# A planned attention and gated-MLP kernel: transposes and quarter loads planned in order of issue, one copy moved, all queues ordered anew

## The chip, the cores and the metric

The kernel runs on one NeuronCore of a Trainium2 chip. The metric is device time in microseconds; the time before is the median of three runs. TensorE is called PE below, VectorE DVE, ScalarE ACT, GpSimd POOL, and SP is the engine that issues most DMAs.

## The reference

The input x has 2048 rows of 512 bf16 numbers. After a LayerNorm without scale, two branches start from the same xn. The first is attention with 32 heads of 16, in which each row looks at 8 rows: itself and those 2, 4, ... 14 before it. The second is a gated MLP of width 1792. The output joins them.

```
xn = layernorm(x)
q, k, v = split(xn @ wqkv)                     # 32 heads of 16
logits[h, s, w] = q[h, s] . k[h, s - 2*w] / 4  # w = 0..7, masked where s - 2*w < 0
o[h, s] = sum over w of softmax(logits)[h, s, w] * v[h, s - 2*w]
s = o @ wo
g = silu( (gelu(xn @ w_gate) * (xn @ w_up)) @ w_down )
out = x + s * g
```

## The kernel before, in words

**Blocks.** The 2048 rows are cut into four blocks of 512 (j = 0 to 3) and sixteen tiles of 128 (t = 0 to 15). For each block the kernel does a LayerNorm, a transpose of xn to columns (`xT`), q, k and v projections, the windowed logits and softmax, the weighted sum of v, the two wide projections gate and up (14 groups of four matmuls each), the down projection (four tiles of 14 matmuls, in pieces of 4, 4, 4 and 2), the output projection (four groups of four matmuls), and the final gating and residual.

**Who does what.** PE does the projections, and the transposes of block 0's four tiles. The transposes of blocks 1 to 3 are DMA transposes on SP's queue (line 393). ACT evicts nearly every PSUM bank (q, k, v at lines 489 and 554 to 563, gelu at 907, up at 915, silu at 973, the output at 1032), takes the exponentials, and for blocks 2 and 3 also the row sums of the LayerNorm (lines 347 and 353). DVE does the products and adds of the attention (741, 754, 834 and around), the gated products (929) and the final gating. POOL issues the stores and loads of v and DMAs that accumulate halves of products (763, 857).

**Through DRAM.** q, k, v and the attention output of a block are stored to DRAM and loaded in another layout: a quarter load brings 128 positions to 32 partitions, so four quarter loads (`ldq`, `ldk` on SP, lines 600 and 618, `ldv` on POOL, line 636) fill a block's tile. `sto` (990) and `ldo` (999) do the same for the attention output, which the output projection reads. Block 0 is apart: its projections go tile by tile (16 matmuls of 128 columns, line 541), so that PE can start after the first tile, and its q and k are used straight from SBUF.

**Tile 0 to 3 at the start.** Each tile is normalised by DVE, transposed by PE into a PSUM bank (`turn`, line 329) and copied into `xT0` (`copy`). The copy of tile 1 is DVE's (line 336), those of tiles 0, 2 and 3 are ACT's (lines 442 and 338).

**What sets the order.** The kernel is written as a list of named operations. Each has an engine, a planned duration, the operations it needs, the buffers it takes and uses, and a priority. `schedule` runs through this list with a model of the engines and queues and picks, for each engine, the ready operation that can start first (within 0.05 us the one of lowest priority number). The result is one order per engine, and the instructions are issued in exactly that order; engines and queues then work in order, and wait on semaphores only for data and buffers. The priorities come from per-block offsets (`N`, `Q`, `S`, `V`, `F`, `Y`, `O` for LayerNorm, projections, logits, values, gate and up, down, output) and from `nudge`, a list with one number for each operation, a tenth of which is added to its priority. The same buffer slots that the plan gives out are used on the chip: six PSUM banks (`F`), one double bank (`L`) for the first two tiles of a down projection, five stores' buffers (`vst`) that the evictions of q, k and v fill in turn, and so on.

**Needs and landings.** In `schedule` an operation becomes ready when all that it needs are done; for a DMA that is its landing. A block's second to fourth transpose name the block's first transpose among their needs, and a block's second to fourth quarter load the first one, because the first takes the buffer:

```
self.op(f"copy{t}", "SP", 1.25, [f"norm{t}"] + ([f"copy{t - tt}"] if tt else []), cross, ...)
need = [f"st_q{j}_{c}" for c in range(NC)] + ([f"ldq{j}_0"] if tq else [])
```

So the plan holds them until the first has landed. **The loads** (`loads`) are a sequence of their own on SP, with priorities from -1000 up, but for the last three (`late=3`: w_down, block 3's x, wo), which need block 1's last norm and have priority 0 and up.

Of the kernel before, what the change touches and what calls it, by code (L numbers as in the profile page):

```python
# [27 lines left out]

B, S, D, DF = 1, 2048, 512, 1792
NC = D // P  # L30
# [24 lines left out]
PARAMS = dict(  # L55
    sums=(2, 3), ladd=2, ln_act=4, warm=4, slack=1.65, N=[-229.9, -416.4, 944.9, 875.4],
    S=[589.3, 14.8, 227.7, 124.2], V=[198.8, 530.8, 849.2, -424.8], Q=[-621.6, -708.7, -247.0, -608.9],
    F=[118.2, 189.7, 347.4, 1042.3], Y=[156.3, 30.0, 947.7, 479.9], O=[-160.4, 783.0, 575.9, 952.0], lsum=(0,),
    late=3, vsum=(0, 1),
    nudge=[  # L60
# [39 lines left out]
    ],  # L100
# [16 lines left out]
def schedule(ops, pools):  # L117
    by = {o.name: o for o in ops}
    assert len(by) == len(ops)
    waits, nexts = {}, {o.name: [] for o in ops}  # L120
    for i, o in enumerate(ops):
        o.n = i
        waits[o.name] = len(o.need)
        for d in o.need:
            nexts[d].append(o.name)
    users = {}
# [17 lines left out]
    while any(ready.values()):  # L144
        best = None
        for e, rs in ready.items():
# [3 lines left out]
            for o in rs:  # L150
                t = max(clock[e], at[o.name])
                ok = True
                if o.take:
                    p, n = o.take[0][0], len(o.take)
                    ok = len(free[p]) >= n
                    if ok:
                        t = max(t, heapq.nsmallest(n, free[p])[-1][0])
# [46 lines left out]
        for n in nexts[o.name]:  # L204
            waits[n] -= 1
            if not waits[n]:
                at[n] = max(
                    by[d].done if by[d].eng == by[n].eng else by[d].end + by[n].slack for d in by[n].need
                )
                ready[by[n].eng].append(by[n])  # L210
# [4 lines left out]
class Kernel:  # L215
# [52 lines left out]
    def layernorm(self, j):  # L268
        base = self.when("N", j)
        for tt in range(TPB):  # L270
# [60 lines left out]
            def copy(t=t, tt=tt, j=j):  # L331
                if tt == 0:
                    self.new(f"xT{j}", [P, NC, TQ], BF16, "xnT")
                out = self.t[f"xT{j}"][:, :, tt * P : (tt + 1) * P]
                if t == 1:
                    self.nc.vector.tensor_copy(out=out, in_=self.t[f"tr{t}"][:])
                else:
                    self.nc.scalar.activation(out=out, in_=self.t[f"tr{t}"][:], func=AF.Copy)
# [49 lines left out]
            if j:  # L388

                def cross(t=t, tt=tt, j=j):  # L390
                    if tt == 0:
# [4 lines left out]

                self.op(f"copy{t}", "SP", 1.25, [f"norm{t}"] + ([f"copy{t - tt}"] if tt else []), cross,
                        take=[("xT", f"xT{j}")] if tt == 0 else [], use=[f"xn{t}", f"xT{j}"], prio=prio,
# [5 lines left out]
            need = [f"turn{t}"] + ([f"copy{t - tt}"] if tt else [])  # L404
            self.op(f"copy{t}", *(("DVE", 0.34) if t == 1 else ("ACT", 0.5)), need, copy, take=take, use=[f"tr{t}", f"xT{j}"], prio=prio)

# [184 lines left out]
    def q_loads(self, j):  # L591
        for tq in range(TPB):
# [11 lines left out]

            need = [f"st_q{j}_{c}" for c in range(NC)] + ([f"ldq{j}_0"] if tq else [])
            self.op(f"ldq{j}_{tq}", "SP", 0.6, need, load, take=[("q", f"q{j}")] if tq == 0 else [],
                    use=[f"q{j}"], prio=1.0, nbytes=260 * 1024, kind="ld")

    def k_loads(self, j):
        for tq in range(TPB):  # L610
# [13 lines left out]
            need += [f"st_k{j - 1}_{c}" for c in range(NC)] if j > 1 else ["st_k0"]  # L624
            need += [f"ldk{j}_0"] if tq else []
            self.op(f"ldk{j}_{tq}", "SP", 0.6, need, load, take=[("k", f"k{j}")] if tq == 0 else [],
                    use=[f"k{j}"], prio=1.0, nbytes=290 * 1024, kind="ld")

    def v_loads(self, j):
        for tq in range(TPB):  # L630
# [11 lines left out]
            if j == 0:  # L642
                need = [f"st_v0_{t}" for t in range(tq + 1)]
            need += [f"ldv{j}_0"] if tq else []
            self.op(f"ldv{j}_{tq}", "POOL", 0.7, need, load, take=[("v", f"v{j}")] if tq == 0 else [],
# [453 lines left out]
    def loads(self, src):  # L1099
# [45 lines left out]
        for i, (name, fn, nbytes) in enumerate(seq):  # L1145
            late = [f"norm{2 * TPB - 1}"] if i >= len(seq) - self.par["late"] else []
            self.op(name, "SP", 0.35, late, fn, prio=(0.0 if late else -1000.0) + i, nbytes=nbytes)

# [117 lines left out]
```

## Time and profile before

| | us |
|---|---|
| median of three runs | 218.44 (216.86 to 218.99) |
| the profiled execution: its time | 218.16 |
| its span in the trace | 216.5 |
| granted TensorE clock, mean | 0.997 |
| PE busy | 207.4 |
| DVE busy | 183.3 |
| ACT busy | 151.4 |
| POOL busy | 44.2 |

The span is the time from the first to the last instruction in the trace of one execution; its time as measured from outside is 1.66 us more. A matmul's busy time is modelled and includes its way through the pipeline (a 512-column matmul shows 379 ns, while the next starts 216 ns after it), so the starts tell more than the busy share. A timeline line gives start, time, engine, line, operation, out<-in and, in brackets, how long the engine stood idle before it and what released it. A line of waits gives who waited for whom, the total, how often, and the longest.

### The profile page before, as it was taken

The numbers are of one execution on the slowest core, as the hardware profiler recorded it, in microseconds if no ns is written. First come the engines' busy times: TensorE is split into PE (matmuls) and PEld (weight loads), VectorE is DVE, ScalarE is ACT, GpSimd is POOL, SyncE is SP. The second block draws the span as 40 slices with busy tenths as digits, with TensorE's granted clock in tenths as the row PEclk, the third lists the DMA queues.
The fourth block names the chain that finished last, engine by engine and source line by source line (L and its number), as shares of the span: only waits on it lengthen the run. The fifth ranks groups of instructions, "written<-read, shape, count | busy, mean of one in ns | idle before, by whom it ended". The sixth has DMA issues, their size and how long they took to land.

```text
span 216.5 us, 3096 instructions
## 1 busy us (share of the span) xinstructions
PE 207.4 (96%) x1108; PEld 99.5 (46%) x1108; DVE 183.3 (85%) x211; ACT 151.4 (70%) x264; POOL 44.2 (20%) x76
## 2 busy tenths in 40 slices
PE   7989999799999999999999999999998999999991
PEld 2986443244444444444444444444443444444440
DVE  4597996499869999789999999997999979999114
ACT  3568999979977997973444797766722787675351
POOL 5209110207091203047001004430210000300000
PEclk9999999999999999999999999999999999999998
DMA  5999999738999944699904638999327052553922
GB/s 161 362 375 358 191 237 307 118 126 206 233 160 246 197 117 140 172 190 232 171 0 97 145 116 225 215 201 188 65 48 181 0 98 96 100 97 65 225 99 97
DMA packets 48623, 36.02 MB, mean 166 GB/s; under 512 B 29904, under 2 KB 45408, under 8 KB 48608
## 3 DMA queue, kind: packets, MB, share of 16 engines
q1 hardware_dynamic: 44240, 23.99, 44.8%
q0 software_dynamic: 4224, 11.78, 26.4%
q8 instruction: 8, 0.13, 0.3%
q14 instruction: 7, 0.06, 0.1%
q10 hardware_dynamic: 144, 0.07, 0.1%
HBM read 17.44 MB, written 9.47 MB: 124 GB/s over the span
## 4 chain that ended last, share of the span: by engine, by line
PE 87%; ACT 4%; DMA 3%; DVE 3%; issue 1%; SPq 0%; DVEq 0%
PE y_ps L955 22%; PE u_ps L891 20%; PE g_ps L891 20%; PE qkv_ps L478 14%; PE s_ps L1018 5%; PE qkv_ps L541 5%; DMA xnT<-xn 2%; DMA x_sb<-in_A_x_dram 1%; ACT gl L907 1%; ACT hT L915 1%; DVE s L1069 1%; ACT junk L347 1%; ACT junk L353 1%; DVE s L1075 1%; DVE stats L413 0%
## 5 line engine op out<-in xcount | busy, mean ns | idle before, releaser
L891 PE MATMUL u_ps<-xnT,wu_sb 128*128 128x512 bf16 x224 | 54.2, 379 | 0.0
L891 PE MATMUL g_ps<-xnT,wg_sb 128*128 128x512 bf16 x224 | 53.9, 379 | 0.0
L955 PE MATMUL y_ps<-wd_sb,hT 128*128 128x512 bf16 x224 | 50.3, 379 | 0.7 <-ACT sil L973 0.7
L907 ACT ACTIVATE gl<-g_ps 128x512 bf16<-128x512 f32 x56 | 32.1, 597 | 15.8 <-PE g_ps L891 11.6
L915 ACT ACTIVATE hT<-u_ps 128x512 bf16<-128x512 f32 x56 | 32.6, 597 | 11.0 <-PE u_ps L891 10.8
L834 DVE TENSOR_TENSOR pv<-attn,v_arr 128x4096 bf16<-128x4096 bf16 x16 | 36.0, 2288 | 0.1
L955 PEld LDWEIGHTS <-hT 128*128 128x128 bf16 x224 | 21.8, 98 | 27.6 <-issue 1.0
L891 PEld LDWEIGHTS <-wu_sb 128*128 128x128 bf16 x224 | 21.9, 98 | 26.4
L891 PEld LDWEIGHTS <-wg_sb 128*128 128x128 bf16 x224 | 21.9, 98 | 26.2
L741 DVE TENSOR_TENSOR prod<-q_sb,k_sb 128x4096 bf16<-128x4096 bf16 x12 | 27.1, 2288 | 3.7 <-DMA k_sb<-kT_dram 2.5
L489 ACT ACTIVATE qkv_st<-qkv_ps 128x512 bf16<-128x512 f32 x36 | 20.6, 598 | 3.2 <-PE qkv_ps L478 3.1
L754 DVE TENSOR_TENSOR prod<-prod 128x1024 bf16<-128x1024 bf16 (+2 forms) x33 | 22.6, 738 | 0.0
L929 DVE TENSOR_TENSOR hT<-hT,gl 128x1024 bf16<-128x1024 bf16 x28 | 18.8, 688 | 2.2 <-ACT hT L915 1.5
L973 ACT ACTIVATE sil<-y_ps 128x512 bf16<-128x512 f32 x16 | 8.8, 596 | 14.0 <-PE y_ps L955 13.9
L857 POOL DMA_DIRECT2D pv<-pv x8 | 7.1, 892 | 52.8 <-DVE pv L834 29.6
L1018 PE MATMUL s_ps<-wo_sb,oT_sb 128*128 128x512 bf16 (+2 forms) x68 | 14.6, 366 | 0.0
L636 POOL DMA_DIRECT2D v_arr<-vT_dram x16 | 11.3, 802 | 15.1 <-DMA vT_dram<-vst 10.7
L478 PE MATMUL qkv_ps<-xnT,wk_sb 128*128 128x512 bf16 x48 | 11.7, 379 | 1.6 <-DMA xnT<-xn 1.6
L496 POOL DMA_DIRECT2D vT_dram<-qkv_st x12 | 7.1, 597 | 27.0 <-ACT qkv_st L489 26.5
L478 PE MATMUL qkv_ps<-xnT,wq_sb 128*128 128x512 bf16 x48 | 11.3, 379 | 0.0
L1032 ACT ACTIVATE s<-s_ps 128x512 bf16<-128x512 f32 x15 | 8.8, 595 | 3.6 <-PE s_ps L1018 3.6
L478 PE MATMUL qkv_ps<-xnT,wv_sb 128*128 128x512 bf16 x48 | 11.2, 379 | 0.0
(89 smaller groups left out, 219.1 us busy)
## 6 DMA issues: line engine op xcount, KB each, us to landing
pv<-pv POOLq DMA_DIRECT2D x8, 512.0 KB, 5.4
v_arr<-vT_dram POOLq DMA_DIRECT2D x16, 142.0 KB, 6.4
oT_dram<-o_sb SPq DMA_DIRECT2D x16, 128.0 KB, 3.0
oT_sb<-oT_dram SPq DMA_DIRECT2D x4, 512.0 KB, 4.4
wg_sb<-in_B_w_gate_dram SPq DMA_DIRECT2D x2, 896.0 KB, 11.1
wu_sb<-in_B_w_up_dram SPq DMA_DIRECT2D x2, 896.0 KB, 13.8
wd_sb<-in_B_w_down_dram SPq DMA_DIRECT2D x1, 1792.0 KB, 10.2
k_sb<-kT_dram SPq DMA_DIRECT2D x12, 142.0 KB, 4.4
```

The lines of the kernel that those rows point to most:

```text
L478: self.nc.tensor.matmul(ps[:], lhsT=self.w_sb[which][:, dk, c * P : (c + 1) * P], rhs=self.t[f"xT{j}"][:, dk, :], start=(dk == 0), stop=(d ...
L489: self.nc.scalar.activation(out=st[:], in_=self.t["ps_" + key][:], func=AF.Copy, scale=SCALE if which == 0 else 1.0)
L636: self.nc.gpsimd.dma_start(out=self.t[f"v{j}"][H * tq : H * (tq + 1), :, :], in_=self.vT.rearrange("(h d) s -> h d s", d=DH)[:, :, a : a + ...
L741: self.nc.vector.tensor_tensor(out=pr[:], in0=self.t[f"q{j}"].unsqueeze(1).to_broadcast([P, 2, DH, P]), in1=win, op=ALU.mult,)
L754: self.nc.vector.tensor_tensor(out=pr[:, :, 0:n, :], in0=pr[:, :, 0:n, :], in1=pr[:, :, n : 2 * n, :], op=ALU.add)
L834: self.nc.vector.tensor_tensor(out=pv[:], in0=self.t[f"at{j}"][:, 2 * i : 2 * i + 2, :].unsqueeze(2).to_broadcast([P, 2, DH, P]), in1=win, ...
L891: nc.tensor.matmul(ps[:], lhsT=w[:, dk, fc * P : (fc + 1) * P], rhs=self.t[f"xT{j}"][:, dk, :], start=(dk == 0), stop=(dk == NC - 1),)
L907: self.nc.scalar.activation(out=self.t[f"gl{j}_{pair}"][:, fc % 2, :], in_=self.t[f"ps_g{j}_{fc}"][:], func=AF.Gelu_apprx_tanh,)
L915: self.nc.scalar.activation(out=self.t[f"h{j}"][:, fc, :], in_=self.t[f"ps_u{j}_{fc}"][:], func=AF.Copy)
L929: self.nc.vector.tensor_tensor(out=h, in0=h, in1=self.t[f"gl{j}_{pair}"][:], op=ALU.mult)
L955: nc.tensor.matmul(self.t["ps_" + key][:, 0 : n1 - n0], lhsT=self.t[f"h{j}"][:, fc, tt * P : (tt + 1) * P], rhs=self.wd_sb[:, fc, n0:n1], ...
L1018: self.nc.tensor.matmul(ps[:, 0 : n1 - n0], lhsT=self.t[f"oT{j}"][:, c, tt * P : (tt + 1) * P], rhs=self.wo_sb[:, c, n0:n1], start=(c == 0 ...
```

## The change

The source changes in four places, and the planner's numbers are new.

- In `schedule`, a need that begins with "~" is met at the start of the named operation and not at its end. The needs of the later DMA transposes and quarter loads on the block's first one are of this kind now.
- The tiles of block 0 whose copy DVE does are a parameter, `vcopy=(1, 2)`; before it was tile 1 alone.
- The three late loads have priorities from 400 up instead of from 0.
- The offsets, `slack` and all of `nudge` are new, so that the order on every engine and queue is another one.

```
-    sums=(2, 3), ladd=2, ln_act=4, warm=4, slack=1.65, N=[-229.9, -416.4, 944.9, 875.4],
+    sums=(2, 3), ladd=2, ln_act=4, warm=4, slack=1.77, N=[-366.5, -394.8, 949.9, 936.2],
...
-    late=3, vsum=(0, 1),
+    late=3, vcopy=(1, 2), vsum=(0, 1),
     nudge=[
...
-            nexts[d].append(o.name)
+            nexts[d.lstrip("~")].append(o.name)
...
                 at[n] = max(
+                    by[d[1:]].start if d[0] == "~" else
                     by[d].done if by[d].eng == by[n].eng else by[d].end + by[n].slack for d in by[n].need
                 )
...
-                if t == 1:
+                if t in self.par["vcopy"]:
                     self.nc.vector.tensor_copy(out=out, in_=self.t[f"tr{t}"][:])
...
-                self.op(f"copy{t}", "SP", 1.25, [f"norm{t}"] + ([f"copy{t - tt}"] if tt else []), cross,
+                self.op(f"copy{t}", "SP", 1.25, [f"norm{t}"] + ([f"~copy{t - tt}"] if tt else []), cross,
...
-            self.op(f"copy{t}", *(("DVE", 0.34) if t == 1 else ("ACT", 0.5)), need, copy, take=take, use=[f"tr{t}", f"xT{j}"], prio=prio)
+            self.op(f"copy{t}", *(("DVE", 0.34) if t in self.par["vcopy"] else ("ACT", 0.5)), need, copy, take=take, use=[f"tr{t}", f"xT{j}"], prio=prio)
...
-            need = [f"st_q{j}_{c}" for c in range(NC)] + ([f"ldq{j}_0"] if tq else [])
+            need = [f"st_q{j}_{c}" for c in range(NC)] + ([f"~ldq{j}_0"] if tq else [])
...
-            need += [f"ldk{j}_0"] if tq else []
+            need += [f"~ldk{j}_0"] if tq else []
...
-            need += [f"ldv{j}_0"] if tq else []
+            need += [f"~ldv{j}_0"] if tq else []
...
-            self.op(name, "SP", 0.35, late, fn, prio=(0.0 if late else -1000.0) + i, nbytes=nbytes)
+            self.op(name, "SP", 0.35, late, fn, prio=(400.0 if late else -1000.0) + i, nbytes=nbytes)
```

The orders that come out differ in these places, among many others (operation names as in the code, engine by engine, before and after):

```
SP, start        before  x0, x1, x2, wv, wk, wq, x3, block 1's x, gate and up weights, block 2's x
                 after   x0, x1, wq, x3, wv, x2, wk, block 1's x, gate and up weights, block 2's x
SP, block 1      before  copy4, ld_wd, ld_x3_3, ld_wo, copy6, copy7, copy5, then block 1's stores of q and k
                 after   copy4, copy5, copy6, copy7, ld_wo, ld_wd, ld_x3_3, then block 1's stores of q and k
PE, start        before  v0_t0, v0_t1, k0_t1, k0_t0, q0_t1, q0_t0, turn2, turn3, k0_t2, ...
                 after   q0_t0, q0_t1, v0_t0, turn3, v0_t1, k0_t0, turn2, k0_t3, v0_t3, q0_t2, ...
PE, block 1      before  23 gate and up groups of block 0, red0 and a piece of y0 ahead of the projections of block 1
                 after   15 gate and up groups ahead of them, red0 near their end
PE, y of block 2 before  ... y2_0 (last piece), y2_1 (four pieces), u3_1, ...
                 after   ... y2_0 (last piece), u3_1, u3_0, y2_1 (last three pieces), y2_3 (last piece), ...
PE, end          before  ... y3_2 (last piece), s3_0, s3_1, s3_3 (320 columns), s3_2, s3_3 (192 columns)
                 after   ... y3_2 (last piece), s3_0, s3_2, y3_1 (last piece), s3_3 (192), s3_1, s3_3 (320)
POOL, start      before  st_v0_0, st_v0_1, ldv0_0, rstd of block 1, st_v0_2, st_v0_3, ldv0_1, ...
                 after   st_v0_0, st_v0_1, st_v0_3, rstd of block 1, st_v0_2, ldv0_0, ldv0_1, ...
DVE, block 0     before  pv0_1, pv0_0, pv0_3, pv0_2, sums of block 0, then the products of block 1
                 after   pv0_3, pv0_2, the products of block 1 mixed with pv0_1, pv0_0 and the sums of block 0
```

More of the change, by code (lines that the diff above doesn't have):

```diff
@@ L55 @@
 PARAMS = dict(
-    sums=(2, 3), ladd=2, ln_act=4, warm=4, slack=1.65, N=[-229.9, -416.4, 944.9, 875.4],
-    S=[589.3, 14.8, 227.7, 124.2], V=[198.8, 530.8, 849.2, -424.8], Q=[-621.6, -708.7, -247.0, -608.9],
-    F=[118.2, 189.7, 347.4, 1042.3], Y=[156.3, 30.0, 947.7, 479.9], O=[-160.4, 783.0, 575.9, 952.0], lsum=(0,),
-    late=3, vsum=(0, 1),
+    sums=(2, 3), ladd=2, ln_act=4, warm=4, slack=1.77, N=[-366.5, -394.8, 949.9, 936.2],
+    S=[441.7, 102.5, 376.9, 191.6], V=[262.4, 571.1, 889.9, -410.3], Q=[-642.4, -759.7, -161.1, -640.1],
+    F=[110.3, 227.6, 420.7, 1077.6], Y=[194.6, 11.0, 945.9, 487.5], O=[-220.1, 790.1, 587.2, 953.3], lsum=(0,),
+    late=3, vcopy=(1, 2), vsum=(0, 1),
     nudge=[
[39 rows of a table removed]
[42 rows of a table added]
     ],
```

81 rows, old and new, of the table nudge are left out of this document.

## The prediction

> **What bounds the kernel now.** I read the page first, then PE's timeline, SP's queue and VectorE's waits.
>
> ```profile
> span 216.5 us, 3096 instructions
> PE 207.4 (96%) x1108; PEld 99.5 (46%) x1108; DVE 183.3 (85%) x211; ACT 151.4 (70%) x264; POOL 44.2 (20%) x76
> PE   7989999799999999999999999999998999999991
> PE 87%; ACT 4%; DMA 3%; DVE 3%; issue 1%; SPq 0%; DVEq 0%
> kT_dram<-k_sb SPq DMA_DIRECT2D x1, 16.0 KB, 9.3
> ```
>
> TensorE is busy 96% of the span and holds 87% of the chain that ended last. The work is fixed, so a new order can win only where PE stands still. Its timeline has three such places between the first projection (6.24) and the last matmul (start 211.70):
>
> ```profile
> 12.56 1.08 ACT L338 ACTIVATE xnT<-tr_ps 128x512 bf16<-128x512 bf16 x2
> 13.20 0.61 PE L541 MATMUL qkv_ps<-xnT,wk_sb 128*128 128x128 bf16 x8 [0.73 <-ACT xnT L338]
> ...
> 41.72 1.02 PE L478 MATMUL qkv_ps<-xnT,wk_sb 128*128 128x512 bf16 x4 [1.56 <-DMA xnT<-xn]
> ...
> 166.45 0.81 PE L955 MATMUL y_ps<-wd_sb,hT 128*128 128x512 bf16 x3 [0.69 <-ACT sil L973]
> ```
>
> Start to start, less the usual spacing (57 ns for 128 columns, 217 for 512), they cost 0.89, 1.72 and 0.85: 3.46 in all. The second comes from SP's queue:
>
> ```profile
> 24.94 1.30 SPq L393 DMA_TRANSPOSE xnT<-xn  x1
> 26.30 0.67 SPq L1126 DMA_DIRECT2D wd_sb<-in_B_w_down_dram  x1
> 27.02 1.06 SPq L1108 DMA_DIRECT2D x_sb<-in_A_x_dram  x1
> 28.13 2.27 SPq L1129 DMA_DIRECT2D wo_sb<-in_A_wo_dram  x1
> 30.44 7.64 SPq L393 DMA_TRANSPOSE xnT<-xn  x3
> ```
>
> Three loads (2.75 MB) stand between the first transpose of block 1 and the other three, which land at 40.5 to 41.5. VectorE is the next engine. Its waits:
>
> ```profile
> DVE s L1069 <- ACT s L1032: 8.8, 1, 8.8
> DVE tot L801 <- ACT attn L795: 5.7, 3, 2.8
> DVE prod L741 <- DMA k_sb<-kT_dram: 2.5, 1, 2.5
> ```
>
> The 8.8 is the wait for the last output; the others show how far it follows ScalarE and the loads.
>
> **PE's floor.** I lay the new order of PE out without a stop: tile groups of 16 matmuls at 0.896, groups of four at 0.864, from 6.24 plus 0.25 for the first matmuls, which are spaced 107 ns. It ends at 208.39, as the old order does. Check: 208.39 + 3.46 = 211.85 is where the last matmul ends in the trace, the span ends 4.65 later (216.5), and the execution took 218.16, that is 1.66 more. The median of the runs is 218.44, so I count from 218.16. If nothing stops PE: 208.39 + 4.65 + 1.66 = 214.7. That ceiling is 3.46, or 1.6%.
>
> **The change, part by part.**
>
> *The "~" dependencies* let the planner start a later transpose or quarter load after the first's issue. On the chip nothing waited here before: in block 3 the second transpose is issued at 113.99 and the first lands at 115.15. So this alone is worth nothing; what counts is the order that comes out.
>
> *Tile 2's copy to VectorE.* One copy leaves ScalarE (about 0.5), where tile 2's copy stood behind the eviction of q (12.06 to 12.66). On VectorE it is one copy of 0.42 (row L336). The new order transposes tile 3 after three tile groups and tile 2 after five, so tile 2's copy ends near 12.0 and its first user is due at 13.2. VectorE's 0.42 hides in the wait before its first full products (1.52 in the trace; longer now, as k of tile 1 is made last, at 18.55). Gain 0.89.
>
> *Block 1 early.* The x loads and weights are reordered and block 1's projections come 15 gate/up groups after the first tiles, due at 30.65 (41.72 before). Block 1's statistics end near 15.2, POOL's rstd (2.6, as before) near 17.9, since no v load stands ahead of it. ScalarE then does four norms of 0.70 among its evictions, the last ending near 25.1. SP issues four transposes at about 1.27 each from 21.7, with no load between them. The data must follow what is in SP's ring: before, block 2's x landed at 25.37, the small k store at 27.77 and the first transpose at 28.21; the next ones landed 0.42 to 0.51 apart. That gives 29.7 against 30.65. Gain 1.72, with 0.9 of cover; I charge 0.2 (bounds 0 and the old 1.72).
>
> *Down projection of block 2.* The next piece into the shared bank now stands behind two up groups (1.73), and the silu before it ends near 163.4 against 164.3 due. Gain 0.85.
>
> *First microseconds.* wq and x tile 3 are now issued ahead of wv. wq lands no later than wv did (6.19). VectorE takes tile 3's statistics (0.68) before it copies tile 1; if the tile lands near 6.3 the copy ends at 7.4, just when it is due. Charge 0.15, bounds 0 and 0.9.
>
> *k stores behind the big loads.* wo, wd and block 3's x now follow the transposes, and the first stores of block 1 follow them in the ring. A 16 KB store needed 9.3 us from issue to landing behind such loads; with nothing ahead a store needs 1.8. ScalarE's evictions of q and k reuse the stores' buffers, so they wait for these landings. The three loads took 11.35 before (28.21 to 39.56): from 29.7 they end at 41.1, the first four stores at 41.6 to 43. The evictions want them from 39.5 on and come up to 2.3 late. PE, whose six banks rotate, then waits 0.7 for q's bank at 41.6 and 0.4 for v's at 48. At the pace of the two 512 KB loads (1.51 and 1.56, after POOL's v loads had landed) the three take 8.4, end at 38.1, and cost nothing. In the new order most v traffic is over by 32, so I take the middle of 0 and 1.1, 0.6. The Trainium skill, "DMA: Bandwidth & Descriptors", section "Queues, rings and completion order", says that each DMA engine takes turns between rows of queues by packet; by that the loads run at full pace once POOL's ring is empty, and the sum would be 0.6 lower, where the old pace makes it 0.5 higher. The trace bears the turn-taking out so far as wd took 8.28 beside the v loads, where its bytes at the later pace need 5.3.
>
> *What else moves in the queues.* The three loads come 2 to 3 later than before, when they began at 26.3. wd is first needed at 49.4 and wo at 109.9; block 3's x is needed by ScalarE's first mean of it, near 41.8, with a landing of 38.1 to 41.1: no charge, but it sits in the same ring as the stores above. On POOL tile 3's v store goes ahead of the first rstd and the v loads behind it; they land by 32 and the first value product starts at 49.5. Block 3's four transposes now stand in SP's queue behind the reload of block 0's output. That reload is issued near 103, the buffer they write comes free at 106.4, they land near 112.8 and are due at 114.65: hidden by 1.8. Block 0's output store, which waits for an accumulating DMA until about 125, now stands ahead of block 3's k loads, and the stores of block 1's output ahead of its q loads. These land near 141 to 143, and VectorE wants them at 145. Before, that wait was 1.1 (DVE prod L741 <- DMA q_sb); if it comes back it falls on VectorE's chain, where the next paragraph has 1 to spare.
>
> *VectorE's chain.* The first block's reduction on PE moves from 35.9 to 40.2, so the softmax weights are ready near 49.5 instead of 45.9 (mask, peak, less 2.8; exp table and exp 2.4 behind ScalarE's queue; sums, reciprocal and scaling 3.2). From there to the last sum of block 3 the work is 12 products and 16 value products at 2.20, 20 adds at 1.14, 9 + 12 + 12 + 12 folds at 1.14, 0.60, 0.34, 0.34, 20 gated products at 0.60, three softmaxes at 6.3 and two gates: 143.0. Before, 142.4 from 45.9 would have ended at 188.3 and ended at 196.86: 8.5 of waits. Now products of the next block and value products stand where the waits for exp and loads were; I find 0.7 behind the accumulating DMA of block 1 (it lands 5.5 to 8.2 after issue, 6.7 of work covers it) and 0.8 at block 3's exp. So the last sum ends near 194.0, its reload lands 9.37 later as before: 203.4, and the output projection is due at 204.5. The same for block 2: 162.9 + 0.7, plus 8.29 as before and 0.4 for a store put in between: 172.3 against 172.97. Both hold by about 1; charge 0.5, bounds 0 and the rival below.
>
> *Tail.* PE now ends with the 320-column part of the last tile and the full tile 1 just before it. Behind PE's end stand a 320-column gate (0.48), a gate (0.41), two adds (0.32, 0.42) where before a gate and two adds stood: 0.25 more.
>
> **Sum:** 218.16 - 3.46 + 0.15 + 0.2 + 0.6 + 0.5 + 0.25 = 216.4.
>
> **Rivals.**
>
> *All covers hold:* only the tail is paid, 215.0. For it: PE had no stop but the three in 205 us. Against: three covers are under 1.
>
> *Transposes late again:* if they land at 32.2 rather than 29.7, PE stops 1.55 instead of the 0.2 charged: 217.8. For it: the old trace has one transpose issue of 4.7, right behind the three loads. Against: the large loads now come after.
>
> *VectorE becomes the bound (slower):* it loses its 3.6 of lead at the first softmax, and if it then waits as much as before (8.5), its last sum ends at 201.0, the reload lands at 210.4, the remaining output groups (3.9) end PE at 214.3, and 214.3 + 4.65 + 0.25 + 1.66 = 220.9. It decides against the old time once the waits pass about 5. For it: 85% busy, every us of wait now counts. Against: the new order puts work in the named waits.
>
> **How the numbers follow.** Forecast 216.4 (own range 215.5 to 217.3): 0.42. All covers hold: 0.18. Transposes late: 0.15. VectorE bound: 0.25. I predict 216.4. The range runs from 214.9 (no charge) to 219.8, which leaves out the worse half of the last case. One per cent, 2.2 us, is about what a measurement tells from no change: faster than that is 0.18 and under half of the forecast, 0.36; slower is most of the last case, 0.21; within 0.43.
>
> **What would show it.** Right: no PE stop near 13; block 1's projections start near 30.7, with the transposes landed before; no silu stop; VectorE's waits between first softmax and last sum under 3. Wrong: a PE stop at block 1's projections, ScalarE held at 39 to 43 by k stores, or output groups of blocks 2 and 3 that wait for their reload.

## Result, and the profile after

| | before | after |
|---|---|---|
| median of 6 runs each | 218.40 us (216.86 to 218.99) | 228.81 us (228.28 to 229.74) |
| profiled execution, its span | 218.16, 216.5 | 228.45, 226.7 |

The ratio is 1.0488, 95% interval 1.0449 to 1.0526: slower by 10.4 us, where 216.4 was forecast. The page of the changed kernel, in the same places as the page before:

```profile
span 226.7 us, 3100 instructions
PE 209.8 (93%) x1108; PEld 101.3 (45%) x1108; DVE 183.4 (81%) x212; ACT 149.3 (66%) x263; POOL 57.5 (25%) x76
PE   7999999999997049999999999999999999999991
...
POOL 5045201404289922225020121161201000200100
PEclk9999999999999659999999999999999999999998
PE 62%; DVE 0%; DVEq 0%; issue 0%
```

The three old stops near 13, 41 and 166 us are gone from PE's row. One new hole stands there in slices 13 to 15, and in slices 12 to 14 POOL, which has little to do, is busy for 8 to 9 tenths. TensorE's and ScalarE's waits and POOL's timeline name it (the group row gives count, busy time and mean ns):

```profile
PE qkv_ps L482 <- ACT qkv_st L493: 10.5, 1, 10.5
ACT xn L324 <- POOL nmr L307: 12.0, 1, 12.0
```
```profile
L303 POOL TENSOR_SCALAR rstd<-mv 128x4 f32<-128x4 f32 x3 | 17.1, 5702 | 8.2 <-ACT junk L357 8.1
```
```profile
63.02 16.72 POOL L303 TENSOR_SCALAR rstd<-mv 128x4 f32<-128x4 f32 x1 [1.92 <-ACT junk L357]
79.83 1.03 POOL L306 TENSOR_TENSOR rstd<-rstd,mhalf 128x4 f32<-128x4 f32 x1
80.94 0.20 POOL L307 TENSOR_TENSOR nmr<-mv,rstd 128x4 f32<-128x4 f32 x1
```

One POOL instruction on 128x4 numbers, the first of `rstd3_` (function `power`), takes 16.72 us; the other two of its group take 0.19 each. ACT's `norm14` waits for the result and stands ahead of the evictions of block 2's q, k and v; PE's banks fill, and it stops from 71.6 to 82.5 us. Followed back by these waits the chain is short: PE, ACT, POOL (the page's own chain ends where the hole ends, and so holds 62% of the span). What holds POOL is not in its row. VectorE's timeline has it, at the instant when POOL's instruction ends:

```profile
75.94 2.29 DVE L838 TENSOR_TENSOR pv<-attn,v_arr 128x4096 bf16<-128x4096 bf16 x1
78.14 0.42 DVE L756 TENSOR_TENSOR Ls<-prod 128x256 f32<-128x256 bf16 x1
78.48 1.22 DVE L845 TENSOR_TENSOR pv<-pv 128x2048 bf16<-128x2048 bf16 x1
79.61 1.87 DVE L780 TENSOR_REDUCE peak<-Ls 128x128 f32<-128x1024 f32 x1
```

From 51.62 to 79.6 VectorE issues nothing but elementwise instructions with both inputs in SBUF, each starting 0.08 ahead of the end of the one before, without a pause. POOL comes through when the reduction begins.

The span's difference, by starts of neighbouring matmuls less their usual spacing: 3.46 of old stops gone, 10.69 of the new stop, 1.31 of half clock behind it (74.998 to 85.24), 1.6 because full clock came at 10.1 us instead of 6.8, 0.2 for a first projection at 6.43 instead of 6.24. That makes 10.3; the spans differ by 10.28 before rounding. In seven more profiles with the same first microseconds full clock came between 4.2 and 7.3, so the 1.6 is that execution's own and no part of the change.

### The profile page after: what moved, and what is told of

The parts are those of the page before. It is cut to its first block, busy times and chain, and to the rows that moved or that the text cites. A ratio compares the mean times of both kernels' runs of the same rounds, so it can differ in the third digit from the quotient of the medians.

```text
span 226.7 us, 3100 instructions
## 1 busy us (share of the span) xinstructions
PE 209.8 (93%) x1108; PEld 101.3 (45%) x1108; DVE 183.4 (81%) x212; ACT 149.3 (66%) x263; POOL 57.5 (25%) x76
## 4 chain that ended last, share of the span: by engine, by line
PE 62%; DVE 0%; DVEq 0%; issue 0%
PE y_ps L959 17%; PE u_ps L895 16%; PE g_ps L895 15%; PE qkv_ps L482 8%; PE s_ps L1022 6%; DVE s L1073 0%; DVEq L1265 0%; DVE s L1079 0%
## 5 line engine op out<-in xcount | busy, mean ns | idle before, releaser
L895 PE MATMUL u_ps<-xnT,wu_sb 128*128 128x512 bf16 x224 | 53.2, 379 | 0.0
L959 PE MATMUL y_ps<-wd_sb,hT 128*128 128x512 bf16 x224 | 52.3, 379 | 0.0
L911 ACT ACTIVATE gl<-g_ps 128x512 bf16<-128x512 f32 x56 | 31.6, 600 | 12.2 <-PE g_ps L895 9.6
L482 PE MATMUL qkv_ps<-xnT,wv_sb 128*128 128x512 bf16 x48 | 12.8, 399 | 10.5 <-ACT qkv_st L493 10.5
L303 POOL TENSOR_SCALAR rstd<-mv 128x4 f32<-128x4 f32 x3 | 17.1, 5702 | 8.2 <-ACT junk L357 8.1
L324 ACT ACTIVATE xn<-x_sb,nmr,rstd 128x512 bf16<-128x512 bf16 x12 | 9.7, 824 | 12.0 <-POOL nmr L307 12.0
L805 DVE TENSOR_TENSOR tot<-attn 128x512 f32<-128x512 bf16 x4 | 2.8, 690 | 14.3 <-ACT attn L799 14.3
L672 DVE TENSOR_TENSOR prod<-q_sb,k_sb 128x1024 bf16<-128x1024 bf16 (+1 forms) x12 | 9.7, 862 | 5.1 <-ACT k_sb L562 5.1
```

Of the source, the lines that this page charges most:

```text
L303: nc.gpsimd.tensor_scalar(out=r, in0=self.mv[:, a:b, 1], scalar1=k, scalar2=EPS, op0=ALU.mult, op1=ALU.add)
L482: self.nc.tensor.matmul(ps[:], lhsT=self.w_sb[which][:, dk, c * P : (c + 1) * P], rhs=self.t[f"xT{j}"][:, dk, :], start=(dk == 0), stop=(d ...
L895: nc.tensor.matmul(ps[:], lhsT=w[:, dk, fc * P : (fc + 1) * P], rhs=self.t[f"xT{j}"][:, dk, :], start=(dk == 0), stop=(dk == NC - 1),)
L911: self.nc.scalar.activation(out=self.t[f"gl{j}_{pair}"][:, fc % 2, :], in_=self.t[f"ps_g{j}_{fc}"][:], func=AF.Gelu_apprx_tanh,)
L959: nc.tensor.matmul(self.t["ps_" + key][:, 0 : n1 - n0], lhsT=self.t[f"h{j}"][:, fc, tt * P : (tt + 1) * P], rhs=self.wd_sb[:, fc, n0:n1], ...
```

## Experiments

The theory at first, A1: POOL's small instruction stays out as long as VectorE issues two-SBUF-input instructions back to back.

**Is it this wait, and is it VectorE?** Block 3's rstd on VectorE:

```
             def power(a, b, k):
+                if a == 3 * TPB:      # nc.vector: tensor_scalar, tensor_tensor
+                    ...
+    before("rstd3_", "fold1_3_4")     # place in the emitted order
```

> The changed kernel with block 3's rstd computed by VectorE, two 128x4 instructions between the products prod1_2 and fold1_3_4, instead of three on POOL. VectorE's form leaves out the power -1/2, so block 3 is scaled by another factor; the time is not touched by that. Theory A (the 16.72 us of POOL's rstd at 63.0 hold ACT's norm14 and so TensorE from 71.6 to 82.5, and VectorE's stream causes them): the stop and the half clock behind it go, 228.4 - 10.7 - 1.3 + 0.3 for VectorE's two instructions = 216.7 us, 215.5 to 218. Rival B (the stop is ACT's or PSUM's own and POOL's wait only falls beside it): a stop of 8 us or more stays, 226 or more. Rival C (the stop goes but later waits take it back, because block 2's copies and VectorE's products only queue elsewhere): 219 to 225.

215.47 us (one run; the kernel before beside it 217.76); no PE stop at 71. The whole loss hangs on this one step, and nothing takes it back later. The second edit leaves POOL's part and puts six tiny reductions into VectorE's order:

```
     for o in order:
+        if o.name in ("fold1_3_4", "fold1_0_4", "fold1_2_8", "fold1_0_2", "fold1_2_4", "fold1_0_1"):
+            nc.vector.tensor_reduce(out=k.spare[:], in_=k.mhalf[:], op=ALU.max, axis=AX.X)
         o.emit()
```

> The changed kernel with POOL's rstd as it is, and six tiny reductions (128x1 from 128x4, f32) put into VectorE's order, one ahead of each of fold1_3_4, fold1_0_4, fold1_2_8, fold1_0_2, fold1_2_4 and fold1_0_1 (65.6 to 69 us). Theory A1 (POOL's small instruction is kept out as long as VectorE issues instructions with two inputs in SBUF without a break, and one reduction lets it in): the first rstd instruction ends at about 65.8, all three by 69.5, no TensorE stop above 2 us at 71, 217 us (216 to 218.5). Rival A2 (POOL gets in only where VectorE's next instruction waits for another engine or a transfer): the reductions wait for nobody, POOL still waits until about 80, 229 us. Rival A3 (POOL is slow through its own work, the accumulating transfer that it issued at 59.8, or ACT's statistics, and VectorE has no part): still about 16 us, 229 us.

214.98 us, one run. POOL's timeline, from the second profile of the same kernel:

```profile
61.48 2.67 POOL L303 TENSOR_SCALAR rstd<-mv 128x4 f32<-128x4 f32 x1 [1.93 <-ACT junk L357]
64.23 1.42 POOL L306 TENSOR_TENSOR rstd<-rstd,mhalf 128x4 f32<-128x4 f32 x1
65.73 0.95 POOL L307 TENSOR_TENSOR nmr<-mv,rstd 128x4 f32<-128x4 f32 x1
```

The three get in beside the reductions, so A2 and A3 fall. Timed again, alone and with more warm-up matmuls:

> The changed kernel with the six tiny reductions, timed again: all three rstd instructions get in at them, as in its first run (214.98 beside 217.76). If the changed plan is right but for the one wait: 215.2 us, 214.7 to 216, a ratio to the kernel before of 0.982 to 0.99. Rival: the first run was a lucky one and POOL is kept out in some runs: times spread up to 229.

215.12 us (214.89 to 215.62), ratio to the kernel before 0.9861, interval 0.9826 to 0.9897: the changed plan without the one wait takes 1.4% less than the kernel before.

```
         if i == 3: two more matmuls of 128x128 into the warm-up tile
```

> The same with two more warm-up matmuls (128x128, 0.1 us each at half clock) behind the eight of 512 columns, so that TensorE pauses 0.05 to 0.2 us instead of 0.28 to 0.41 ahead of the first transposes. If that pause let the clock come late in the changed kernel's profiled run (full clock at 10.1 us, in the kernel before at 6.8): full clock by 7.3 us or before, 0.2 to 0.8 us less in the median than without. Rival (the instant of the clock's grant is the run's own and only 128 columns more change nothing): within 0.3 us of the run without.

215.82 us, ratio 0.9882 (0.9842 to 0.9921), full clock at 7.03 against 6.66 without. There is no gain, so the pause ahead of the transposes is not shown to be what delays the clock; the rival's "within 0.3 us" is missed too, by a median 0.7 higher, with intervals that overlap.

**Does the old order starve POOL too?** In the kernel before:

```
+        if o.name == "rstd3_":                  # now behind prod1_2
+            nc.vector.memset(k.mhalf[:], -0.5)
```

> The kernel before, with one edit: VectorE sets the constant that block 3's second rstd instruction (the power) reads anew behind prod1_2, so that the power becomes due at about 67.8, inside VectorE's run of products and folds, instead of 60.2. Theory A1: the power is kept out until VectorE runs dry, which is at geglu1_0 (78.4), whose inputs come from ACT, and ACT stands at norm14: 10 to 11 us, TensorE stops 8 to 11 us with its buffers full, 226 to 231 us in the kernel before. Rival A2: it gets in at 75.6 to 76, at the fold whose order has a wait for another engine: 8 us, 223 to 227. Rival A3: it takes 1 to 2 us, norm14 is 3 us late and most of that is hidden, 218 to 220.5.

224.07 us, but not by the cause that A1 gave. POOL's timeline:

```profile
67.78 2.94 POOL L302 TENSOR_TENSOR rstd<-rstd,mhalf 128x4 f32<-128x4 f32 x1 [4.79 <-DVE mhalf L1239]
70.79 1.29 POOL L303 TENSOR_TENSOR nmr<-mv,rstd 128x4 f32<-128x4 f32 x1
```

The power (1.04 alone) lost 1.9, up to the boundary between two products, both of two SBUF inputs. Most of the time goes to the later due time itself: ACT waited 7.3 for it, PE stopped for 3.6 and then lost 1.7 in 3.4 us at half clock. By the wait A3 was right; the time lies in A2's range, but for another reason. So here, where VectorE had stood still until 65.3, its run lets POOL in at the first boundary. A1 was incomplete.

**What decides whether POOL gets in.** Bare runs: VectorE repeats one instruction, and POOL asks with a 128x4 instruction.

> Nothing of the reference is computed: twelve stretches, each a run of 8 to 28 VectorE instructions of one kind, and beside it POOL's three small rstd instructions (128x4, f32), due when the run's first instruction starts. Theory A1: in the runs with two SBUF inputs (bf16 2048; the same with a long-met wait on ACT; with a long-met wait on a transfer; a dependent chain; f32 1024; bf16 256) the first POOL instruction takes until the run's end, 8 to 10 us; in the runs with one input in PSUM, copies, one input, or reductions 0.2 us; with a tiny reduction or memset behind each instruction each POOL instruction waits for one of them, 1 to 1.5 us. Rival A2: with waits on ACT or on a transfer the POOL instruction gets in within 1 to 2.5 us, and in the dependent chain as well; else as A1. Rival A3: 0.2 us in all twelve.

All three theories miss. POOL's first instruction got in behind the running instruction in nearly every stretch; in one it stayed out, 9.04 us. Beside reductions or an input in PSUM it took 0.19.

> Nothing of the reference is computed. The first such run had one stretch of twelve in which POOL's 128x4 instruction stayed out for all of VectorE's eight instructions (9.04 us), the one whose inputs a transfer had loaded into the upper part of SBUF; in the others with two SBUF inputs it got in behind the first instruction (1.1 to 1.2 us). So the run's kind alone does not decide. Here are 30 stretches of the same eight instructions (128x2048 bf16, two inputs in SBUF), with one input from one tile at a middle place, from eight tiles at a low place or from eight at a high place, the first two with waits on loads, and POOL held back by a memset of 0 to 56 elements. Place (the addresses decide): the high place stays out for 8 to 9 us every time, the others 1.2 us at most. Waits (the loads' waits decide): only the two stretches with waits on loads stay out. Instant (when POOL asks within VectorE's steps decides): some of each place stay out, some not, and with the hold-back it changes; the four repeats without hold-back give mixed waits.

Neither place, nor waits, nor instant: it alternates. POOL's timeline, stretches 2 to 5 (the idle in brackets is POOL's):

```profile
37.17 1.09 POOL L61 TENSOR_SCALAR r<-m 128x4 f32<-128x4 f32 x1 [26.99 <-DVE m L55]
...
46.32 9.04 POOL L61 TENSOR_SCALAR r<-m 128x4 f32<-128x4 f32 x1 [6.92 <-DVE m L55]
...
56.09 0.93 POOL L61 TENSOR_SCALAR r<-m 128x4 f32<-128x4 f32 x1
...
65.24 8.87 POOL L61 TENSOR_SCALAR r<-m 128x4 f32<-128x4 f32 x1
```

A stretch in which POOL stays out ends with VectorE waiting for POOL (0.37 us), and the next one, begun from a standstill, is open. A stretch in which POOL gets in is followed without a pause, and the next is shut. Hence the age theory. The shift of the instant in the kernel itself says the same:

```
+        if o.name == "rstd3_":
+            nc.gpsimd.memset(k.junk[:], 0.0)
```

> The changed kernel with one POOL instruction more: a memset of 128x512 bf16 that waits for the same statistics and stands ahead of block 3's rstd, so that the rstd asks some tenths of a us later; VectorE's order is the same. Theory A1 as first stated (VectorE's unbroken run keeps POOL out whatever the instant): rstd still waits until the reduction at about 79.6, 228.5 us. Instant theory (a request at another moment within VectorE's steps gets in behind the running instruction): the three rstd instructions take 1 to 2.5 us each, the TensorE stop at 71 goes, 215 to 217.5. If the memset itself is kept out, that speaks for A1 and against a fault of the one instruction: 228.5 too.

228.59 us. The memset took 0.53 beside VectorE's run; the rstd behind it, which now asks 0.22 us into a VectorE instruction instead of 0.79, took 16.14. An instruction that only writes gets through, one that reads does not.

> Nothing of the reference is computed. In the second such run POOL's instruction got in behind the first VectorE instruction (0.9 to 1.1 us) and stayed out to the end (8.9 to 9.0 us) in strict turn, whatever the place or the instant; each stretch in which it got in began where VectorE had just stood still, each in which it stayed out began without a pause behind an earlier run. Here 21 stretches all begin with a pause of VectorE (a round trip over ACT); POOL asks behind instruction k of a run of 128x2048 instructions. Age theory (open while the run is young since its last pause or other instruction, shut when it is old): for k = 1 about 1.1 us; from some k between 2 and 9 on, to the run's end, 5.7 us for k = 9 of 14 and 3.4 us for 11 of 14; with a tiny reduction, memset, one-input instruction or an instruction that reads the one before, put in before or behind the request, 1 to 2.5 us. Turn theory (it gets in every second time): in and out alternate over the first eight stretches whatever k. Theory A1 (only another kind of instruction lets it in, at the moment when it comes): out to the end for every k, from 14 us at k = 1 down to 3.4 us, and a reduction ahead of the request does not help. For f32 1024 and bf16 256 as for the long bf16 ones, for one input in PSUM 0.2 us; copies and one-input f32, unknown: 0.2 to 6 us.

POOL's timeline, each stretch 14 long instructions unless said otherwise:

```profile
64.39 1.10 POOL L59 TENSOR_SCALAR r<-d 128x4 f32<-128x4 bf16 x1 [16.43 <-DVE d L81]
81.93 10.19 POOL L59 TENSOR_SCALAR r<-d 128x4 f32<-128x4 bf16 x1 [16.43 <-DVE d L86]
100.60 7.92 POOL L59 TENSOR_SCALAR r<-d 128x4 f32<-128x4 bf16 x1 [8.48 <-DVE d L91]
...
168.60 5.64 POOL L59 TENSOR_SCALAR r<-d 128x4 f32<-128x4 bf16 x1 [10.82 <-DVE d L115]
185.00 1.10 POOL L59 TENSOR_SCALAR r<-d 128x4 f32<-128x4 bf16 x1 [10.75 <-DVE d L122]
201.71 1.10 POOL L59 TENSOR_SCALAR r<-d 128x4 f32<-128x4 bf16 x1 [15.61 <-DVE d L127]
...
295.60 1.79 POOL L59 TENSOR_SCALAR r<-d 128x4 f32<-128x4 bf16 x1 [5.59 <-DVE d L161]
305.69 0.19 POOL L59 TENSOR_SCALAR r<-fd 128x4 f32<-128x4 f32 x1 [8.31 <-DVE fd L166]
320.60 6.59 POOL L59 TENSOR_SCALAR r<-d 128x4 f32<-128x4 bf16 x1 [14.72 <-DVE d L171]
335.56 6.59 POOL L59 TENSOR_SCALAR r<-fd 128x4 f32<-128x4 f32 x1 [8.37 <-DVE fd L176]
```

Row by row: asked behind instruction 4 after a pause, POOL is in at the next boundary (1.10; the same for 1, 2 and 3). Behind 5 it is out to the end (10.19), and so behind 7 (7.92), 9 and 11. With a reduction directly ahead of the request (168.60): still out. With a reduction while POOL waits (185.00): in. With a seventh instruction that reads the sixth, and the request behind the ninth (201.71): in. Behind 25 instructions of 256 columns it is out to the end (1.79). The last rows: with one input in PSUM POOL is in at once; copies and a one-input f32 instruction shut it out like the others.

Whether the number of instructions or the time since the pause decides is left open by these rows. Counted from the first instruction behind the pause, the request behind four long ones comes at 4.70 us and gets in, the one behind 25 short ones at 5.22 and the one behind five long ones at 5.84 stay out, so a limit of about 5 us would do as well as a limit of four. Earlier runs fit neither. In the first bare run a request during the tenth of the 256-column instructions, 1.84 us behind the first, got in (101.42 to 101.75), which a limit of four forbids; in the kernel before with the late rstd its last instruction asked at 70.79, 5.32 us into VectorE's run, and got in at the boundary at 72.0, which a limit below 5.22 forbids. In both POOL had been let in just before, and whether that makes the run young was not tested. A third case stays unexplained: in the first bare run a request behind nine copies, without a pause of VectorE since the first of them 10.5 us earlier, got in at the next boundary (0.56 us).

The two kernels with one reduction, built before that was known:

```
-    gaps = (... six ...)
+    gaps = ("fold1_3_8",)       # the other kernel: ("fold1_3_4",)
```

> The changed kernel with a single tiny reduction in VectorE's order, ahead of fold1_3_8 (62.2 us), so 0.8 us before POOL's rstd asks; VectorE's run since 51.6 us is thereby cut before the request and not behind it. Age theory: the first rstd instruction gets in at the next boundary (63.4), the others within 5 us, no TensorE stop, 215 to 216 us. Theory A1 (only a break that comes while POOL waits): still held until 79 to 80 us, 228.5 us.

> The changed kernel with a single tiny reduction ahead of fold1_3_4 (65.6 us), while POOL's first rstd instruction waits. Age theory: it lets the first in (at about 65.6 less the lead of the run) and, the run being young again, the other two at the boundaries behind, all by 68.5; no TensorE stop above 1 us, 215 to 216 us. Theory A1: the first instruction gets in there, the power asks at once and is then held until the reduction at 79 us: 227 to 228.5 us.

229.3 and 228.14 us, one run each; the age theory as it then stood missed both, and A1 had both right. POOL's timeline of the second:

```profile
61.74 2.68 POOL L303 TENSOR_SCALAR rstd<-mv 128x4 f32<-128x4 f32 x1 [1.93 <-ACT junk L357]
64.50 14.86 POOL L306 TENSOR_TENSOR rstd<-rstd,mhalf 128x4 f32<-128x4 f32 x1
```

The reduction at 64.28 lets the first in; the power, which asks at 64.50, is out until the reduction of `peak1`. As in the bare run, a reduction opens only for its own moment and does not make the run young. What does, in the bare run, is VectorE running empty, and an instruction that has to wait for its predecessor is enough. So two neighbours are exchanged, to let a fold follow the fold that it reads:

```
+    before("fold1_3_4", "prod1_2")
```

> The changed kernel with two neighbours of VectorE's order exchanged: fold1_3_4 ahead of prod1_2 instead of behind it, so that it stands directly behind fold1_3_8, whose result it reads. No instruction is added. Age theory as the third bare run left it (POOL gets in for about five instructions after VectorE has run empty, a reduction opens only for its own moment, and an instruction that waits for the one before makes VectorE run empty): fold1_3_4 waits for fold1_3_8 at 63.4 us, just after POOL asks at 63.0; the three rstd instructions get in at the next three boundaries, done by 67 us, no TensorE stop above 1 us at 71, 215 us (214.5 to 216), ratio 0.982 to 0.991. Theory A1 (only another kind of instruction lets it in): held until 79 to 80 us, 228 to 229.

215.83 us (214.87 to 216.59), ratio 0.9886, interval 0.9847 to 0.9925. POOL's timeline:

```profile
63.18 0.48 POOL L303 TENSOR_SCALAR rstd<-mv 128x4 f32<-128x4 f32 x1 [1.92 <-ACT junk L357]
63.74 1.49 POOL L306 TENSOR_TENSOR rstd<-rstd,mhalf 128x4 f32<-128x4 f32 x1
65.30 1.29 POOL L307 TENSOR_TENSOR nmr<-mv,rstd 128x4 f32<-128x4 f32 x1
```

The first fold ends at 63.605 and the second starts at 63.639: a pause of 0.034 us removes 16 us of waiting, with no instruction added. Here A1, which had 228 to 229, falls. The kernel before shows the same pattern, unread: its rstd asked at 59.32, in an addition that had just waited for its predecessor (58.82 to 58.857), and all three got in at the next boundaries.

**The copy of tile 2**, on top of that version:

```
-                if t in self.par["vcopy"]:
+                if t == 1:          # in copy's emit alone; the order stays
```

> The same, with the copy of tile 2's transpose issued on ACT at the same place of the emitted order, instead of VectorE. The prediction had put 0.89 us of gain to this copy. If it is the engine that brought it: a TensorE stop of 0.5 to 0.9 us near 13 to 15 us, 215.6 to 216 us. If it is the order around it, in which two more projections stand between the transposes of tile 2 and their first reader: the copy ends at about 14.3 behind ev_k0_0, ahead of the reader at 14.9, no stop, within 0.3 us of the run without.

215.72 us, ratio 0.9894 (0.9862 to 0.9927). PE has no stop behind tile 2's transposes (12.20 to 12.6); ACT's copy ends at 13.48, ahead of its first reader at 14.21. (PE's stop of 0.67 right ahead of them, at 11.28, is a wait for the load of wk.) In the new order the copy's engine makes no difference; the order is enough.

## Why the prediction was wrong, by its steps

**The step that failed: POOL's rstd of block 3 has no term in the sum.** The prediction costs "POOL's rstd" only for block 1 ("2.6, as before"), and follows POOL's queue for the v loads. That block 3's rstd now asks at 63.0, in the eighth instruction of a run of VectorE that began at 51.6, was never looked at. The trace before had the warning: its three instructions took 0.82, 1.90 and 0.82 in block 3, against 0.19, 1.04 and 0.20 in block 2, where VectorE was idle. The Trainium skill, "SBUF — State Buffer", section "Who interferes with whom", says that a VectorE instruction with two SBUF inputs and a GpSimd instruction that reads SBUF exclude each other, and that reductions and GpSimd's pure writes are free of it. The runs agree (0.19 beside reductions, 0.53 for the memset). It would have named the risk. By its wording the one that issues first holds the ports for its whole instruction, which by the trace would be the rest of one instruction, an estimate of 0.4 us; measured were that one and 19 more, 16.72 us, and the measurement decides.

**The rest of the sum was 1.4 us too high, because most of its charges did not fall due.** It can be read in the version with six reductions (profiled 214.89, span 213.2), where the wait is gone:
- Three stops, -3.46: gone; behind the first projections no two matmuls stand more than 0.25 us further apart than usual. But the 0.89 near 13 does not need the copy's new engine, to which the prediction put it down.
- Block 1's transposes, charge 0.2: landed at 30.54 (forecast 29.7), projections at 30.79, stop 0.21. The cover is as thin as feared: in the profile with the exchanged folds the transposes land at 32.25 and the same place stops PE for 1.95, the rival "transposes late"; with rstd on VectorE they land at 31.13 and the stop is 0.84.
- k stores, charge 0.6: the first four land at 39.9 to 40.9, PE does not stop; 0. The large loads ended at 39.6, between the two ends.
- VectorE's chain, charge 0.5: the last sum ends at 193.73 (forecast 194.0), the waits since the first softmax are 0.52 (before 8.15); 0.
- First microseconds, 0.15: no stop seen; tail, 0.25: 4.59 from the modelled end of the last matmul against 4.51 before, so 0.08. (The prediction's 211.85 for that end is 211.95 in the trace's row; its sum does not depend on it.)

218.16 - 3.46 + 0.2 + 0.08 = 215.0, the rival "all covers hold", which got 0.18. The rival on the slower side looked for VectorE as the bound. VectorE was indeed the cause, not by its length but by keeping POOL out; of the signs named as "wrong", ACT was held, yet at 69 to 81 by a norm and not at 39 to 43 by stores.

## What to carry to other kernels

When an order is changed, look up for each small POOL instruction that reads SBUF what VectorE runs when it becomes due, and what stands behind its result. An instruction of 0.2 us that took 0.8 in one place of the trace was here already waiting at VectorE's boundaries. If VectorE is in a long run there, let one of its instructions, near the moment when POOL asks, follow the one that it reads; that pause is 0.03 us.

## What the runs showed of the hardware

- A run of VectorE without a pause kept a read of POOL out across 20 instructions, 16.72 us here. It does not at first: in the third bare run POOL gets in at a boundary for requests up to 4.70 us (four long instructions) behind the run's start, and from 5.22 us (25 short ones) on not at all. Whether the number or the time decides, and whether letting POOL in starts the count again, stays open.
- A pause of 0.034 us opens it again (16.72 us became 0.48); a reduction opens it for its own moment alone (the next request took 14.86).
- Copies and one-input f32 instructions shut POOL out as well (6.59 us each, to the end of their run); a memset of POOL's own, which only writes, took 0.53 us inside VectorE's run.
- Full TensorE clock came between 4.2 and 10.1 us in executions with the same warm-up.
